# 99 units kept between two layers, and a ring of 14 units instead of 16

## The chip, the cores and the metric

The kernel runs on one core of one Trainium2 chip. The metric is the time of one execution on the device in microseconds. Three runs of the kernel before took 2572.51, 2572.63 and 2572.84 us; the median is 2572.63 us.

## The reference

Two layers with the same weights, one after the other, for two sequences of one new token each. A layer is a grouped-query attention over a cache and then a gated feedforward, each with a layer norm ahead and a residual around it:

```python
q = (x @ wq).reshape(B, Sq, Hq, Dh)                     # 32 query heads, 8 key heads, Dh 128
scores = einsum("bhqd,bhkd->bhqk", q, k) * Dh ** -0.5   # 32768 keys
o = einsum("bhqk,bhkd->bhqd", softmax(scores), v)
x = x + o @ wo
h = gelu(x @ w_gate) * (x @ w_up)                       # 512 -> 1792
x = x + h @ w_down
```

Everything is float32. Keys and values of both sequences are 537 MB, and a layer reads all of them, so the two layers read them twice unless something of the first pass is still on the chip when the second begins.

## The kernel before

**Units and places.** The on-chip memory is one tile `M` of 110 units; a unit is 128 partitions x 512 floats, 262,144 bytes. Units 0 to 31, 32 to 63 and 64 to 95 are three slots (A, B, C) for half a head's keys or values of one sequence (32 units). Units 96 to 107 are the zone for weights; 106 and 107 also hold the exponentials of the attention, 108 and 109 their transposes and other short-lived data.

**What sets the order of transfers.** All loads go through one list, `plan`, in the order in which they are needed. `pump` (L107) issues them on SyncE's queue from the head of the list while the units that the head wants are free; a head that has to wait holds back all behind it. `free` (L125) is called after the instructions that read a unit last, and calls `pump`. So transfers run in order, and each is issued as soon as its place has been read for the last time. TensorE consumes the units in the same order.

**The turn between the layers.** Layer 1 walks the pairs of head and sequence backwards, so the last pair of layer 0 is the first of layer 1, and what of its keys and values is still in `M` is not loaded again. Before the change these are 97 units: both value halves (64), the first `KC1` = 28 units of the second key half, which stay in slot C, and the last `NPS` = 5 units of the first key half (27 to 31), which are copied to PSUM banks ahead of the softmax (L500, L505) and later back to `M` by `store` (L537). The other 4 units of the second key half are loaded again as ("k1",), the other 27 of the first as ("k0", 1).

**The ring.** While those units are held, the weights of feedforward 0 (gu 28 units, wd 14) and the query weights of layer 1 (wq7 4 units, then wq 28) pass through what is left: 16 units in four places of 4, used in the order 104, 92, 96, 100 (`RING`, `PL`, `ring_stream` L166). The place 92 lies in slot C, behind the 28 kept units. A transfer into a place waits for the products that read its occupant.

**The consumers.** `feedforward(0)` makes 28 products from gu (L403), the gelu, and 14 products from wd (L452). Then `center` (L262) normalises, and `query_unit` (L281) makes the query of head 7 from wq7. After that seven groups m = 0 to 6 follow: each makes 4 query products for the other heads (L281, bank 7) and then scores four kept key units (L305, bank 5), in `early` portions of 0, 4, 4, 4, 4, 4 and the rest. Each scored key unit is freed for the first key half of the same pair, which comes as transfers of 8, 8, 8 and 3 units. Behind the groups stand the query copy and gather of all other heads (L285, L289), the scores of the reloaded k1 units and the scores of the first key half, in which the units that were kept in PSUM come after the first 24.

Of the kernel before, what the change touches and what calls it, by code (L numbers as in the profile page):

```python
# [28 lines left out]
CH = 32  # L29
# [3 lines left out]

NU = 110
SLOT_A, SLOT_B, SLOT_C, ZONE = 0, 32, 64, 96
PL = [96, 100, 104, 92]
U_P0, U_P1, U_PT = 106, 107, 108
XW = 46
XO = 14
# [4 lines left out]
NPS = 5  # L44
KFREE = CH - NPS
RING = [2, 3, 0, 1]
KC1 = 28
NARROW = [6, 1]
NH = 2
NG = P // 16  # L50
# [24 lines left out]
def block_kernel(ctx: ExitStack, tc: tile.TileContext, x, consts, kt, vt, wq, wo, wn, gu, wd, out):  # L75
# [28 lines left out]
    def add(key, src, u, n):  # L104
        plan.append((key, src, u, n))
# [30 lines left out]
    def cols(a, lo, n):  # L136
        return a[:, lo * U:(lo + n) * U]
# [17 lines left out]
    def stream(name, l, src, total, cuts, places):  # L155
        lo = 0
        where = {}
        for n, u in zip(cuts, places):
            add((name, l, lo), cols(src, lo, n), u, n)
            for i in range(n):  # L160
                where[lo + i] = ((name, l, lo), u + i)
            lo += n
        assert lo == total
        pieces[(name, l)] = where

    def ring_stream(name, l, src, total, at):  # L166
        cuts, places, n = [], [], 0
        while n < total:
            cuts.append(min(4, total - n))
            places.append(PL[RING[at % 4]])  # L170
            n += 4
            at += 1
        stream(name, l, src, total, cuts, places)

# [14 lines left out]
    for l in range(2):  # L189
        if l == 0:  # L190
            stream("wq", 0, wq, 32, (16, 16), (SLOT_C, SLOT_C + 16))
            ring = [SLOT_A, SLOT_B, SLOT_C]
            todo = sequence(orders[0], 0)
            roles = [ring[(len(todo) - 4 + i) % 3] for i in range(3)]
        else:
            last0, last1, lastv = roles
            ring = [lastv, last0, last1]
            g, b = orders[1][0]
            assert last1 == SLOT_C
            add(("wq7",), cols(wq, 28, 4), ZONE + 2, 4)  # L200
            stream("wq", 1, wq, 28, (4, 2, 2, 4, 4, 4, 2, 2, 4), [ZONE + i for i in (6, 10, -4, -2, 2, 6, 10, -4, -2)])
            add(("k1",), cols(kt[b, g, 1], KC1, CH - KC1), ZONE + 2, CH - KC1)
            stream("k0", 1, kt[b, g, 0], KFREE, (8, 8, 8, 3), [last1 + i for i in (0, 8, 16, 24)])
            g, b = orders[1][1]
            chunk("k", 1, g, b, 0, last1, (8, 8, 16))
            chunk("k", 1, g, b, 1, lastv, (16, 16))
            chunk("v", 1, g, b, 0, last0)
            add_wo(1, g)
            chunk("v", 1, g, b, 1, last1)
            todo = sequence(orders[1][2:], 1)  # L210
        for i, (g, b, nm_, h) in enumerate(todo):
            if nm_ == "w":
                add(("wn", l, g), wn[l], ring[i % 3], NC)
                continue
            last = i == len(todo) - 1
            second = (g, b) == orders[l][orders[l].index((g, b))] and orders[l].index((g, b)) % 2 == 1
            if nm_ == "v" and h == 1 and second and not last:
                add_wo(l, g)
            chunk(nm_, l, g, b, h, ring[i % 3], (8, 8, 8, 4, 4) if last else (CH,))
            if last:  # L220
                add_wo(l, g)
        if l == 0:
            ring_stream("gu", 0, gu, 28, 0)
            ring_stream("wd", 0, wd, 14, 7)
        else:
            stream("gu", 1, gu, 28, (8, 8, 8, 4), [ring[(len(todo) - 3) % 3] + 8 * i for i in range(4)])
            stream("wd", 1, wd, 14, (4, 4, 2, 2, 1, 1), [ring[(len(todo) - 2) % 3] + i for i in (0, 4, 8, 10, 12, 13)])
# [75 lines left out]
    def score_unit(S, w, i, u, start, stop):  # L303
        c, t = divmod(i, 4)
        nc.tensor.matmul(S[32 * t:32 * t + 32, :], w[:, 28 - 4 * c:60 - 4 * c], mem(u), start=start, stop=stop)  # L305
# [215 lines left out]
    g, b = last  # L521
# [7 lines left out]
    k1 = pieces[("k", 0, g, b, 1)]  # L529
    where = pieces[("wq", 1)]  # L530
    S0, S1, A1 = bank[0], bank[5], bank[1]
    todo, s = deque(range(KC1)), 0
    early = [0, 4, 4, 4, 4, 4, CH]
    C0 = SLOT_C + KFREE
    held = {30: C0 + 1, 31: C0 + 2, 27: C0 + 3, 28: C0 + 4, 29: C0}
# [5 lines left out]
    for m in range(7):  # L541
        for j in range(4):
            key, u = where[s]
            at(key)
            query_unit(X, m, j, u, m == 0, m == 6)
            s += 1
        for j in range(4):
            free(where[s - 4 + j][1])
        if m == 0:
            query_gather(mem(U_PT), Q7, 7, 1)  # L550
            w = window(g, b)
        for j in range(min(early[m], len(todo))):
            i = todo.popleft()
            score_unit(S1, w, i, k1[i][1], i < 4, False)
            free(k1[i][1])
        if m == 5:
            store(30, True)
            store(31, False)
    store(27, True)
    store(28, False)  # L560
    store(29, True)
    restart()
    query_copy(X, mem(U_PT + 1))
# [2 lines left out]
    where = pieces[("k0", 1)]  # L566
    u = at(("k1",))
    for i in range(KC1, CH):
        score_unit(S1, w, i, u + i - KC1, False, True)
    free(u, CH - KC1)  # L570
    peak(S1, 1)
    seq = list(range(24)) + [30, 31, 27, 28, 29] + [24, 25, 26]
    left = {i % 4: i for i in seq}
# [67 lines left out]
```

## Time and profile before

| | |
|---|---|
| median of three runs | 2572.63 us |
| the profiled execution | 2573.33 us, of it the span 2571.2 us |
| PE busy | 1359.9 us (53%) |
| DVE, ACT busy | 139.1 us (5%), 83.5 us (3%) |
| read from HBM | 1103.98 MB, 429 GB/s over the span |
| SyncE's DMA queue | 99.6% of the 16 engines' span |
| granted TensorE clock, mean | 0.742 |

The span is the time from the first to the last instruction. In the answers for windows the columns after the stretch are the busy times of PE, of its weight loads, DVE, ACT and POOL with their numbers of instructions, then the granted clock, the DMA share and GB/s. A float32 product over one unit stands as two instructions in the trace, so "x8" is four units. In rows of the timeline the two numbers ahead are start and duration, and the bracket behind says how long the engine sat idle before and what ended that.

### The profile page before, as it was taken

The page shows a single profiled execution, that of the slowest core. Times are in us where ns is not written, and L with a number is a line of the kernel's source. Part 1 is how long each engine was busy: PE and PEld are TensorE (multiplying, and loading weights), DVE is VectorE, ACT ScalarE, POOL GpSimd, SP SyncE. Part 2 cuts the span into 40 slices and gives each one's busy share as a digit, 9 for nine tenths or more (in the row PEclk, how much of TensorE's full clock was granted, in tenths as well). Part 3 has the DMA queues.
Part 4 walks back from the last instruction along what each step waited for, and adds up shares of the span by engine and source line. Part 5 has one row for each costly group of instructions (what it writes and reads, how often), then busy time and mean ns, then how long its engine had stood idle before and what let it go on. Part 6 is the DMA issues. An engine that isn't in the chain of part 4 may idle for free.

```text
span 2571.2 us, 20235 instructions
## 1 busy us (share of the span) xinstructions
PE 1359.9 (53%) x9444; PEld 385.1 (15%) x9444; DVE 139.1 (5%) x459; ACT 83.5 (3%) x191; POOL 3.8 (0%) x12
## 2 busy tenths in 40 slices
PE   4554545555445554464576454454455544554556
PEld 1111111111111111111122111111111111111112
DVE  0000000000000000000011000000000000000001
ACT  0000000000000000000010000000000000000000
POOL 0000000000000000000000000000000000000000
PEclk8777777777777777777798777777766777777778
DMA  9999999999999999999999999999999999999998
GB/s 425 426 436 437 428 436 431 433 431 438 428 435 434 429 436 429 436 430 435 423 408 438 431 432 437 426 436 433 431 436 431 434 432 435 428 437 431 434 429 368
DMA packets 27771, 1105.34 MB, mean 430 GB/s; under 512 B 3208, under 2 KB 3464, under 8 KB 5000
## 3 DMA queue, kind: packets, MB, share of 16 engines
q1 hardware_dynamic: 27400, 1103.97, 99.6%
q8 instruction: 74, 1.21, 0.2%
q10 hardware_dynamic: 288, 0.09, 0.0%
q14 instruction: 9, 0.07, 0.0%
HBM read 1103.98 MB, written 0.07 MB: 429 GB/s over the span
## 4 chain that ended last, share of the span: by engine, by line
DMA 67%; PE 23%; another core or an unknown queue 9%; issue 0%; ACT 0%; DVE 0%; SPq 0%; DVEq 0%
DMA M<-in_vt 57%; PE bank L350 16%; DMA M<-in_kt 7%; PE bank L305 5%; DMA M<-in_gu 3%; DMA M<-in_wq 1%; PE bank L371 0%; PE bank L403 0%; DMA M<-in_wd 0%; ACT M L359 0%; PE bank L361 0%; PE bank L452 0%; PE bank L333 0%; DVE oT L364 0%
## 5 line engine op out<-in xcount | busy, mean ns | idle before, releaser
L305 PE MATMUL bank<-M,qw 128*32 128x512 f32 x4096 | 589.2, 737 | 546.8 <-DMA M<-in_kt 546.8
L350 PE MATMUL bank<-M 128*16 128x512 f32 x4096 | 583.9, 733 | 508.4 <-DMA M<-in_vt 508.4
L305 PEld LDWEIGHTS bank<-M,qw 128*32 128x32 f32 x4096 | 142.8, 132 | 980.4 <-DMA M<-in_kt 584.6
L350 PEld LDWEIGHTS bank<-M 128*16 128x16 f32 x4096 | 137.4, 112 | 928.2 <-issue 914.3
L308 DVE TENSOR_REDUCE sm<-bank 128x1 f32<-128x512 f32 x64 | 44.3, 692 | 1124.9 <-PE bank L305 1124.9
L330 ACT ACTIVATE M<-bank,sm 128x512 f32<-128x512 f32 x64 | 43.4, 683 | 1230.7 <-DVE sm L325 1230.7
L333 PE MATMUL bank<-cst,M 128*128 128x128 f32 x256 | 51.1, 348 | 42.3 <-ACT M L330 42.0
L364 DVE TENSOR_REDUCE oT<-bank 128x4 f32<-128x64 f32 x32 | 7.2, 225 | 1120.6 <-PE bank L361 1120.6
L359 ACT ACTIVATE M<-bank,sm 128x512 f32<-128x512 f32 x32 | 22.0, 687 | 1139.2 <-PE bank L350 1139.2
L334 DVE COPY M<-bank 128x512 f32<-128x512 f32 x64 | 43.9, 692 | 60.8 <-PE bank L333 60.8
L333 PEld LDWEIGHTS bank<-cst,M 128*128 128x128 f32 x256 | 37.0, 176 | 52.6 <-ACT M L330 52.6
L361 PE MATMUL bank<-cst,M 128*128 128x128 f32 x128 | 21.0, 286 | 25.9 <-ACT M L359 25.9
L403 PE MATMUL bank<-M,xw 128*32 128x512 f32 x112 | 24.4, 830 | 10.7 <-DMA M<-in_gu 10.1
L324 PE MATMUL bank<-cst,sm 128*128 128x128 f32 x32 | 10.3, 323 | 35.1 <-DVE sm L323 35.1
L338 PEld LDWEIGHTS bank<-cst,sm 128*128 128x128 f32 x128 | 23.1, 253 | 0.0
L361 PEld LDWEIGHTS bank<-cst,M 128*128 128x128 f32 x128 | 13.4, 140 | 55.3 <-ACT M L359 55.3
L338 PE MATMUL bank<-cst,sm 128*128 128x4 f32 x128 | 21.1, 270 | 0.0
L281 PE MATMUL bank<-M,xw 128*32 128x512 f32 x128 | 19.0, 673 | 3.1 <-DMA M<-in_wq 2.4
L371 PE MATMUL bank<-M,oT 128*2 128x512 f32 x120 | 16.6, 592 | 5.1 <-DVE oT L364 5.1
L259 PE MATMUL bank<-cst,xin 128*2 128x128 f32 x32 | 5.0, 308 | 23.2 <-DMA cst<-in_consts 23.2
L324 PEld LDWEIGHTS bank<-cst,sm 128*128 128x128 f32 x32 | 4.3, 133 | 64.2 <-DVE sm L323 64.2
L330 ACT ACTIVATION_READ_ACCUMULATOR M<-bank,sm 128x1 f32 x64 | 12.5, 196 | 0.0
(73 smaller groups left out, 136.3 us busy)
## 6 DMA issues: line engine op xcount, KB each, us to landing
M<-in_wo SPq DMA_DIRECT2D x14, 1024.0 KB, 51.0
M<-in_vt SPq DMA_DIRECT2D x6, 2048.0 KB, 43.1
M<-in_kt SPq DMA_DIRECT2D x3, 4096.0 KB, 19.5
M<-in_kt SPq DMA_DIRECT2D x5, 2048.0 KB, 13.6
M<-in_wq SPq DMA_DIRECT2D x2, 4096.0 KB
M<-in_gu SPq DMA_DIRECT2D x8, 1024.0 KB, 8.6
M<-in_wq SPq DMA_DIRECT2D x6, 1024.0 KB, 7.9
M<-in_gu SPq DMA_DIRECT2D x3, 2048.0 KB, 37.8
```

Source lines behind the costliest of these rows:

```text
L281: nc.tensor.matmul(Q[32 * k:32 * k + 32, :], xw[:, k, XO - 2 * g:XO - 2 * g + 32], mem(u), start=start, stop=stop)
L305: nc.tensor.matmul(S[32 * t:32 * t + 32, :], w[:, 28 - 4 * c:60 - 4 * c], mem(u), start=start, stop=stop)
L308: nc.vector.tensor_reduce(mx[:, h:h + 1], S, axis=AX.X, op=OP.max)
L330: nc.scalar.activation(p[h], S[h], AF.Exp, bias=bias, scale=SCALE, accum_out=ls[:, h:h + 1])
L333: nc.tensor.transpose(S[h][:, k * P:(k + 1) * P], p[h][:, k * P:(k + 1) * P], ident)
L334: nc.vector.tensor_copy(mem(U_PT + h), S[h])
L338: nc.tensor.matmul(X[:, P:P + REP], ls[:, h:h + 1].to_broadcast([P, P]), mask, start=(h == 0), stop=(h == 1))
L350: nc.tensor.matmul(acc[32 * t:32 * t + 16, :], mem(U_PT + h)[:, k * P + 32 * t + 16 * e:k * P + 32 * t + 16 * e + 16], mem(u), start=(h == ...
L359: nc.scalar.activation(md, acc, AF.Copy, scale=linvc)
L361: nc.tensor.transpose(X[:, c * P:(c + 1) * P], md[:, c * P:(c + 1) * P], ident)
L371: nc.tensor.matmul(W[32 * t:32 * t + NB, :], oT[:, t, :], mem(u + t - lo), start=(t > 0 and first), stop=final)
L403: nc.tensor.matmul(G[v][32 * t:32 * t + 32, :], xw[:, k, XO:XO + 32], mem(un), start=(k == 0), stop=(k == KC - 1))
```

## The change

99 units are kept: `KC1` is 30, so 30 units of the second key half stay in slot C, and two instead of four are loaded again. Two units less are left for the ring, which now has places of 4, 2, 4 and 4 units at 104, 94, 96 and 100 (`SIZE`). gu passes in pieces of 4, 2, 4, 4, 4, 2, 4, 4, and wd in 4, 2, 4, 4. wq7 and wq get other places in the same units, and so other occupants to wait for.

```diff
-PL = [96, 100, 104, 92]
+PL = [96, 100, 104, 94]
+SIZE = [4, 4, 4, 2]
-KC1 = 28
+KC1 = 30
@@ ring_stream
-            cuts.append(min(4, total - n))
-            places.append(PL[RING[at % 4]])
-            n += 4
+            i = RING[at % 4]
+            cuts.append(min(SIZE[i], total - n))
+            places.append(PL[i])
+            n += SIZE[i]
             at += 1
@@ the plan of layer 1
-            add(("wq7",), cols(wq, 28, 4), ZONE + 2, 4)
-            stream("wq", 1, wq, 28, (4, 2, 2, 4, 4, 4, 2, 2, 4), [ZONE + i for i in (6, 10, -4, -2, 2, 6, 10, -4, -2)])
-            add(("k1",), cols(kt[b, g, 1], KC1, CH - KC1), ZONE + 2, CH - KC1)
+            add(("wq7",), cols(wq, 28, 4), ZONE + 8, 4)
+            stream("wq", 1, wq, 28, (4, 4, 4, 2, 2, 4, 4, 4), [ZONE + i for i in (-2, 2, 6, 10, -2, 0, 4, 8)])
+            add(("k1",), cols(kt[b, g, 1], KC1, CH - KC1), ZONE - 2, CH - KC1)
...
-            ring_stream("wd", 0, wd, 14, 7)
+            ring_stream("wd", 0, wd, 14, 8)
@@ the turn between the layers
-    todo, s = deque(range(KC1)), 0
+    first = [*range(18), 28, 29, *range(18, 28)]
+    ends = {i % 4: i for i in [*first, 30, 31]}
+    todo, s = deque(first), 0
...
-            score_unit(S1, w, i, k1[i][1], i < 4, False)
+            score_unit(S1, w, i, k1[i][1], i < 4, ends[i % 4] == i)
...
-    store(27, True)
-    store(28, False)
     store(29, True)
...
     for i in range(KC1, CH):
-        score_unit(S1, w, i, u + i - KC1, False, True)
+        score_unit(S1, w, i, u + i - KC1, False, ends[i % 4] == i)
     free(u, CH - KC1)
+    store(27, True)
+    store(28, False)
     peak(S1, 1)
```

The units that come back from PSUM go to 91 to 95. Before, 92 to 95 were ring units by then. Now 92 and 93 are kept key units 28 and 29, which are therefore scored by group 5, ahead of `store(30)` and `store(31)`; and 94 and 95 hold the reloaded k1 units, so `store(27)` and `store(28)` stand behind their scores.

SyncE's queue from the output projection of layer 0 to the first key half of layer 1, before (128x512 is one unit, so 128x2048 is four):

```order
L119 DMA M<-in_wo 128x2048
L119 DMA M<-in_gu 128x2048 x7
L119 DMA M<-in_wd 128x2048 x3
L119 DMA M<-in_wd 128x1024
L119 DMA M<-in_wq 128x2048 x2
L119 DMA M<-in_wq 128x1024 x2
L119 DMA M<-in_wq 128x2048 x3
L119 DMA M<-in_wq 128x1024 x2
L119 DMA M<-in_wq 128x2048
L119 DMA M<-in_kt 128x2048
L119 DMA M<-in_kt 128x4096 x3
```

and in the changed kernel:

```order
L120 DMA M<-in_wo 128x2048
L120 DMA M<-in_gu 128x2048
L120 DMA M<-in_gu 128x1024
L120 DMA M<-in_gu 128x2048 x3
L120 DMA M<-in_gu 128x1024
L120 DMA M<-in_gu 128x2048 x2
L120 DMA M<-in_wd 128x2048
L120 DMA M<-in_wd 128x1024
L120 DMA M<-in_wd 128x2048 x2
L120 DMA M<-in_wq 128x2048 x4
L120 DMA M<-in_wq 128x1024 x2
L120 DMA M<-in_wq 128x2048 x3
```

The pieces are cut otherwise, with the same sums for gu, wd and wq; the row that follows there is `M<-in_kt 128x1024`, two units where four stood.

PE at the end of the groups, before (bank 7 collects the queries, bank 5 the scores of the second key half, bank 0 those of the first; L259 and L289 are the residual and the query gather):

```order
L281 MATMUL bank7_81<-M_63,xw_65 32x512 x4
L305 MATMUL bank5_79<-M_63,qw0_66 32x512 x8
L259 MATMUL bank6_80<-cst_64,xin_73 2x128 x4
L289 MATMUL bank7_81<-cst_64,M_63 128x14 x4
L305 MATMUL bank5_79<-M_63,qw0_66 32x512 x4
L305 MATMUL bank0_74<-M_63,qw0_66 32x512 x32
```

and in the changed kernel, where the same lines are numbered two higher:

```order
L283 MATMUL bank7_81<-M_63,xw_65 32x512 x4
L307 MATMUL bank5_79<-M_63,qw0_66 32x512 x10
L261 MATMUL bank6_80<-cst_64,xin_73 2x128 x4
L291 MATMUL bank7_81<-cst_64,M_63 128x14 x4
L307 MATMUL bank5_79<-M_63,qw0_66 32x512 x2
L307 MATMUL bank0_74<-M_63,qw0_66 32x512 x32
```

Two of the 32 scores moved from behind the gather to ahead of it.

ScalarE in the same place, before (L285 copies the queries, L539 is `store`):

```order
L285 COPY M_63<-bank5_79 128x512
L539 COPY M_63<-bank0_74 128x512
L539 COPY M_63<-bank2_76 128x512
L539 COPY M_63<-bank4_78 128x512
L285 COPY M_63<-bank7_81 128x512
```

and in the changed kernel:

```order
L287 COPY M_63<-bank5_79 128x512
L543 COPY M_63<-bank0_74 128x512
L543 COPY M_63<-bank4_78 128x512
L287 COPY M_63<-bank7_81 128x512
L543 COPY M_63<-bank2_76 128x512
```

The copy from bank 2, which is unit 27, moved behind the query copy; on VectorE the copy from bank 3, unit 28, moved likewise behind the query gather's scaling and ahead of the maximum of the second key half.

## The prediction

> **What bounds the kernel now.** I read the page's head first, for the DMA share, then its chain of waits, then the stage that the change touches (from about 1262 us to 1375 us) by windows and by timeline.
>
> ```profile
> span 2571.2 us, 20235 instructions
> DMA  9999999999999999999999999999999999999998
> DMA packets 27771, 1105.34 MB, mean 430 GB/s; under 512 B 3208, under 2 KB 3464, under 8 KB 5000
> q1 hardware_dynamic: 27400, 1103.97, 99.6%
> DMA 67%; PE 23%; another core or an unknown queue 9%; issue 0%; ACT 0%; DVE 0%; SPq 0%; DVEq 0%
> ```
>
> The transfer engines are busy in all forty slices, and the one queue of SyncE fills 99.6% of their time with 1103.97 MB. PE is on the chain with 23%, but only as what frees a buffer for the next transfer. So the time is bytes over rate, and a change counts if it alters the bytes or lets the queue run dry. The stage between the layers is no exception:
>
> ```profile
> 1289.00:1336.00 47.00, 35.38 (x244) 10.31 (x240) 7.81 (x34) 5.63 (x13) 1.70 (x3) 0.93 1.00 405
> 600.00:800.00 200.00, 103.07 (x723) 29.09 (x719) 11.14 (x35) 5.72 (x14) 0.00 (x0) 0.74 1.00 433
> ```
>
> The last two columns are the DMA share and GB/s. The ring stage has a share of 1.00 like the attention stage, at 405 against 433 GB/s: never dry, a little slower per byte. Single arrivals there can be read off PE, which waits for each piece:
>
> ```profile
> 1293.04 1.06 PE L403 MATMUL bank<-M,xw 128*32 128x512 f32 x8
> 1295.52 1.94 PE L403 MATMUL bank<-M,xw 128*32 128x512 f32 x8 [1.41 <-DMA M<-in_gu]
> 1305.43 1.47 PE L403 MATMUL bank<-M,xw 128*32 128x512 f32 x7 [0.57 <-DMA M<-in_gu]
> 1324.31 1.07 PE L281 MATMUL bank<-M,xw 128*32 128x512 f32 x8 [0.56 <-DMA M<-in_wq]
> 1334.56 1.07 PE L281 MATMUL bank<-M,xw 128*32 128x512 f32 x8 [0.55 <-DMA M<-in_wq]
> ```
>
> From 1293.04 to 1305.43 five pieces of 4 units arrive, 2.48 us each, so 0.62 us a unit; from 1324.31 to 1334.56 sixteen units, 0.64 us each. PE needs 1.06 us for 4 units at the full clock and 1.94 us at half; the windows inside those two rows show the clocks (the figure ahead of the last two):
>
> ```profile
> 1293.10:1294.00 0.90, 0.90 (x8) 0.10 (x8) 0.02 (x2) 0.00 (x0) 0.70 (x1) 1.00 1.07 428
> 1295.60:1297.40 1.80, 1.80 (x8) 0.12 (x8) 0.00 (x0) 0.00 (x0) 0.00 (x0) 0.50 1.01 414
> ```
>
> **The change part by part.** *The two units.* The last kt transfer of the old second key half shrinks from 4 units to 2. All other sizes add up as before, so 2 x 262,144 bytes leave the queue. At 0.62 to 0.64 us a unit that is 1.24 to 1.28 us, at the page's 430 GB/s 1.22 us. I take **1.25 us**, since the transfer lies in this stage. The number of transfers from wo up to the first 8-unit kt piece is the same (7 + 4 + 10 + 1 = 22 before, 8 + 4 + 9 + 1 = 22 now), so a cost per transfer would not move.
>
> *Does the gain reach the end?* After the ring the first key half streams in:
>
> ```profile
> 1341.94 1.92 PE L305 MATMUL bank<-M,qw 128*32 128x512 f32 x16 [1.32 <-DMA M<-in_kt]
> 1346.84 3.54 PE L305 MATMUL bank<-M,qw 128*32 128x512 f32 x16 [2.98 <-DMA M<-in_kt]
> 1351.75 3.68 PE L305 MATMUL bank<-M,qw 128*32 128x512 f32 x32 [1.37 <-DMA M<-in_kt]
> 1373.62 38.25 DMA M<-in_vt
> ```
>
> PE waits 1.32 us for the first piece of it. Arriving 1.25 us sooner uses that up almost wholly, but PE still waits 2.98 us at the next piece, so the end of the key half, and with it the softmax, the 128 value products and the vt transfer of 1373.62, come 1.25 us sooner with the queue. That vt transfer took 38.25 us to land for about 20 us of its own bytes, so nothing runs dry there.
>
> *The smaller ring.* A transfer is safe while enough is queued ahead of it. The page gives issue to landing:
>
> ```profile
> M<-in_gu SPq DMA_DIRECT2D x8, 1024.0 KB, 8.6
> M<-in_wq SPq DMA_DIRECT2D x6, 1024.0 KB, 7.9
> M<-in_wd SPq DMA_DIRECT2D x5, 1024.0 KB, 8.3
> ```
>
> Less its own 2.48 us, a 4-unit piece had 5.4 to 6.1 us of work ahead of it. A ring shorter by two units leaves 4.2 to 4.9 us. What is needed shows only at the start of the program, where the queue is empty: the first row is the first issue, the others are the packets from 0.7 to 1.7, to 1.8 and to 2.8 us:
>
> ```profile
> 0.73 0.86 SPq L119 DMA_DIRECT2D M<-in_wq  x2
> DMA packets 0, 0.00 MB, mean 0 GB/s; under 512 B 0, under 2 KB 0, under 8 KB 0
> DMA packets 3, 0.10 MB, mean 89 GB/s; under 512 B 0, under 2 KB 0, under 8 KB 0
> DMA packets 16, 0.52 MB, mean 250 GB/s; under 512 B 0, under 2 KB 0, under 8 KB 0
> ```
>
> So the first packets start 1.0 us after the issue, and all 16 engines have one about 2.0 us after it. I take 2.0 us as the need; 4.2 us covers it.
>
> *The narrowest place* is the third wq piece. Before, wq7 lay on 98 to 101, and 16 units (wq7 and the four pieces behind it) could be issued ahead of the second normalisation. Now wq7 lies on 104 to 107, and the piece for 102 to 105 must wait until wq7's products are done. Only 12 units (wq7 and two pieces) are ahead: 12 x 0.62 = 7.4 us from the landing of the last wd piece. What runs in that time:
>
> ```profile
> 1314.19 0.09 PEld L452 LDWEIGHTS bank<-M,hT 128*2 128x2 f32 x2 [1.07 <-DMA M<-in_wd]
> 1316.46 0.60 ACT L264 ACTIVATE M<-bank 128x512 f32<-128x512 f32 x1 [6.86 <-PE bank L452]
> 1318.41 1.07 PE L281 MATMUL bank<-M,xw 128*32 128x512 f32 x8 [0.43 <-DVE xw L269]
> 1319.54 0.33 SPq L119 DMA_DIRECT2D M<-in_wq  x1
> ```
>
> Before, the landing is at 1314.19 and the release at 1319.54, 5.35 us later. The landing does not move in the new kernel (46 units from wo to wd in both), but its last piece has 4 units, 1.1 us of PE at the full clock, 1.9 at half. From the normalisation to the release stand 1319.54 - 1316.46 = 3.1 us. So the release comes 4.2 to 5.0 us after the landing, and 7.4 less that leaves **2.4 to 3.2 us** ahead (before, with 16 units: 9.9 - 5.35 = 4.6 us). That is above 2.0, so I price the stall at nothing; the cover is wq7 and the two pieces behind it. The later pieces (released by query products, then four score products) keep some 3.7 us.
>
> The other side of the bound: the trace shows no piece with less than 4.6 us ahead, so by it alone 4.6 could be needed. Then the narrow place loses up to 2.2 us, the three turns of the ring before it, at 4.2 us, 0.4 each, and the one and a half behind it, at 3.7 us, 0.9 each: 4.8 us in all, and with the 1.25 saved 2576.2. I keep to the start of the program, since it shows the very thing, and leave this end a small chance.
>
> The Trainium skill, in DMA: Bandwidth & Descriptors, "Anatomy of one DMA", puts about 2.0 us of fixed cost on a transfer and bytes over 436 GB/s on top (fitted there on GpSimd's path). If the queue paid that per piece, 1 MB would take about 4.4 us by an estimate from that page; this trace has 2.48 us, so it is hidden behind the pieces queued ahead. Where only 2.4 us are queued the rule leaves 0.4 us to spare, and the sum would stay the same by either.
>
> *The moved work.* The scores of the kept units are the same 32, two of them moved from behind the query gather to the last group: 2 x 0.27 = 0.5 us later for the gather, 0.5 us less after it. The copies of units 27 and 28 move behind the last of them, because units 94 and 95 are now theirs after the transfer:
>
> ```profile
> 1335.68 0.69 DVE L539 COPY M<-bank 128x512 f32<-128x512 f32 x1 [1.77 <-PE bank L281]
> 1337.43 0.59 ACT L539 COPY M<-bank 128x512 f32<-128x512 f32 x1 [1.21 <-PE bank L305]
> 1340.68 0.69 DVE L308 TENSOR_REDUCE sm<-bank 128x1 f32<-128x512 f32 x1 [0.66 <-PE bank L305]
> ```
>
> On ACT one 0.59 us copy goes behind the query copy, with nothing waiting behind it until the exponentials. On DVE a 0.69 us copy goes ahead of the maximum of 1340.68, which then ends about 1342.1; its reader, the softmax, starts after the other maximum, behind products that run from 1351.75 to 1355.4. The copied units are read after 24 others, past 1351. Both have some 10 us of cover: **0**. Without it, they would cost 1.3 us.
>
> **Sum:** profiled execution 2573.33 us (span 2571.2 and 2.1 us around it) - 1.25 = 2572.1, span 2569.95. That execution lies 0.70 us above the median of the timed runs, 2572.63, so the forecast for the median is **2571.4 us**, 0.05% less.
>
> **The rivals.** *The narrow place runs dry once.* If a free ring place needs a microsecond more than the start of the program shows, because the engines are loaded, the third wq piece leaves a hole of about 1.2 us and the saving is gone: 2572.6. For it: 2.4 us is a lead that no row shows to be enough. Against: share 1.00 throughout, and 1 to 2 us at the start.
>
> *Slower: the ring starves at half clock.* The windows granted 0.60 at 1312 to 1315 us, 0.83 to 1318, 1.00 after that:
>
> ```profile
> 1312.00:1315.00 3.00, 1.99 (x10) 0.36 (x12) 0.17 (x1) 0.00 (x0) 0.00 (x0) 0.60 1.02 419
> 1315.00:1318.00 3.00, 2.14 (x10) 0.69 (x6) 0.10 (x1) 0.69 (x2) 0.00 (x0) 0.83 1.01 410
> 1318.00:1321.00 3.00, 2.59 (x21) 0.90 (x21) 0.76 (x7) 0.59 (x1) 0.69 (x1) 1.00 1.01 408
> ```
>
> PE has 2.1 us of work (four query and four score products) for every 4 units, which arrive in 2.56. In a window of 3 us at half clock it does 1.5 us of that work where 2.5 are due, and falls 1.0 us behind. The 0.4 us to spare at the narrow place and the 1.25 saved are gone in the second such window, and from there it decides; three of them in a row make a hole of 3.0 - 0.4 = 2.6 us, 1.35 more than is saved: 2572.63 + 1.35 = **2574.0 us**. Against it: PE has more to do just there now (four instead of two units behind the last wd landing), and the clock came back in time before. The Trainium skill, TensorE: Matmul & The Clock Gate, Part 1, gives 1.2 against 2.4 GHz and about 3.4 us of sustained work to come back; 1.94 against 1.06 us agree with the ratio, and by that rule one stretch is the likely length, not three.
>
> *The change does not do what it says,* the two units being loaded elsewhere: 2572.6. The order of SyncE's transfers excludes it, so 1%.
>
> **How the numbers follow.** Forecast 0.75 (2570.9 to 2571.9), dry once 0.12, starving 0.06, not done 0.01, the far bound of 2576.2 0.03; 0.03 for a gain over 2 us that I cannot name. Runs of this kernel agree within 0.33 us, and the profiled one lay 0.7 us above them. The range goes from 2570.3 (1.28 saved, and a microsecond of such difference) to 2573.5, which takes in the first rival with that difference and leaves out starving, the far bound and the unnamed gain, 12 in 100. About 0.2%, 5.1 us, is what a measurement of this kernel can tell from no change; neither 1.25 us saved nor 3.5 lost comes near, so same 0.97, faster 0.01, slower 0.02.
>
> **What would show it.** Right: HBM read 1103.46 MB; DMA share 1.00 from 1289 to 1336 us; the first products of the key half 1.2 us sooner than 1341.94; the third wq transfer after wq7 landing about 5 us after its issue. Wrong: a landing there that comes later than the pieces queued ahead account for, PE waiting over 3 us for in_wq, or a clock of 0.5 past 1318 us.

## The result, and the profile after

The changed kernel takes 2575.4 us, the median of 21 runs from 2572.10 to 2580.14; the kernel before, run beside it, takes 2572.51 us (21 runs, 2572.01 to 2575.8). The ratio is 1.0013, 95% interval 1.0007 to 1.0018. The change costs some 3 us where 1.25 us less was forecast. That is within the 0.2% named beforehand as no change, but outside the predicted range of 2570.3 to 2573.5.

The head of the page after, of an execution of 2578.63 us. The GB/s row has 40 slices of 64.4 us; the ring is in the 21st.

```profile
span 2576.7 us, 20229 instructions
GB/s 424 436 427 435 432 432 435 430 438 428 433 436 430 433 435 428 435 432 434 417 363 430 440 431 433 432 434 431 435 435 429 434 434 430 435 433 430 434 434 367
...
HBM read 1103.45 MB, written 0.07 MB: 428 GB/s over the span
```

The bytes fell as worked out, from 1103.98 to 1103.45 MB. The 21st slice moves 363 GB/s, the lowest of all forty; the slices around it have 417 and 430. The same stretch as in the prediction, in a window and then in pieces of 3 us (the last three columns are the granted clock, the DMA share and GB/s):

```profile
1289.00:1336.00 47.00, 36.01 (x196) 11.63 (x188) 6.79 (x32) 4.68 (x11) 1.69 (x3) 0.76 0.93 349
...
1288.00:1291.00 3.00, 2.12 (x10) 0.11 (x8) 0.22 (x1) 0.49 (x1) 0.00 (x0) 0.50 0.74 304
1291.00:1294.00 3.00, 2.39 (x14) 1.45 (x14) 0.70 (x6) 0.20 (x2) 0.00 (x0) 0.50 0.95 354
1294.00:1297.00 3.00, 3.00 (x18) 1.02 (x14) 0.33 (x3) 0.00 (x0) 0.69 (x1) 0.50 0.66 213
...
1300.00:1303.00 3.00, 1.92 (x12) 0.14 (x4) 1.44 (x4) 1.32 (x3) 0.00 (x0) 1.00 0.74 262
...
1330.00:1333.00 3.00, 3.00 (x24) 0.68 (x20) 0.00 (x0) 0.00 (x0) 0.00 (x0) 0.66 0.90 317
```

Before, these 47 us had a share of 1.00, 405 GB/s and a clock of 0.93. Now the transfer engines run dry again and again, and TensorE is at half clock for long stretches from 1288 us on. 349 in place of 405 GB/s over 47 us are 6.5 us of transfer; the profiled execution lies 7.2 us over the forecast of 2571.4. So the loss is in this stage. The chain of waits through it (start, length, what; a DMA row runs from issue to landing):

```profile
1288.56 1.93 PE bank L373 x8
...
1292.95 1.94 PE bank L405 x8
...
1295.40 3.11 PE bank L405 x14
1298.53 7.38 DMA M<-in_gu
1305.95 3.63 PE bank L405 x10
1309.61 5.63 DMA M<-in_wd
...
1316.35 8.29 DMA M<-in_wq
...
1332.74 5.83 DMA M<-in_wq
```

In this stage PE and the queue release each other in turn: products at half clock (1.93 and 1.94 us for 4 units) free a place late, the transfer into it starts late, the next products wait for it. The timeline of PE shows the largest of these holes and the start of the key half:

```profile
1301.05 1.05 PE L405 MATMUL bank<-M,xw 128*32 128x512 f32 x4 [0.19 <-DMA M<-in_gu]
...
1305.95 5.25 PE L405 MATMUL bank<-M,xw 128*32 128x512 f32 x14 [3.85 <-DMA M<-in_gu]
...
1348.82 1.74 PE L307 MATMUL bank<-M,qw 128*32 128x512 f32 x8 [0.54 <-DMA M<-in_kt]
```

The piece of 1298.53 follows the one that PE takes at 1301.05. It was issued 2.5 us before that landed, a lead that the prediction took for safe, and needs 2.48 us for its own bytes. It is there at 1305.95, 4.90 us after the other: **2.4 us of nothing**. The first full key piece comes at 1348.82; in the profile before it was 1341.94.

Below, the *lead* of a transfer is the time from its issue to the landing of the last piece ahead of it, and a *hole* is what its landing comes later than that piece's landing plus its own bytes.

### The profile page after: what moved, and what is told of

It reads as the page before. It is cut to its first block, busy times and chain, and to the rows that moved or that the text cites. A ratio compares the mean times of both kernels' runs of the same rounds, so it can differ in the third digit from the quotient of the medians.

```text
span 2576.7 us, 20229 instructions
## 1 busy us (share of the span) xinstructions
PE 1362.8 (53%) x9444; PEld 386.1 (15%) x9444; DVE 138.9 (5%) x459; ACT 83.4 (3%) x191; POOL 3.8 (0%) x12
## 2 busy tenths in 40 slices
DMA packets 27771, 1104.82 MB, mean 429 GB/s; under 512 B 3208, under 2 KB 3464, under 8 KB 5128
## 3 DMA queue, kind: packets, MB, share of 16 engines
HBM read 1103.45 MB, written 0.07 MB: 428 GB/s over the span
## 4 chain that ended last, share of the span: by engine, by line
DMA 64%; PE 24%; another core or an unknown queue 10%; ACT 1%; issue 0%; DVE 0%; SPq 0%; DVEq 0%
DMA M<-in_vt 55%; PE bank L352 16%; DMA M<-in_kt 6%; PE bank L307 6%; DMA M<-in_gu 2%; DMA M<-in_wd 1%; DMA M<-in_wq 1%; PE bank L373 1%; ACT M L361 0%; PE bank L363 0%; PE bank L386 0%; PE bank L405 0%; PE bank L283 0%; PE bank L335 0%
```

## The experiments

All times are medians (range of the runs) beside the kernel before in the same session, which took 2572.46, 2572.75 and 2572.67 us. All ratios are to it, with 95% intervals.

### The changed kernel once more

No edit.

> The changed kernel once more, unaltered, to see its spread and a second profile. Theory A (TensorE at half clock reads the ring's pieces late, the clock windows lie otherwise in each run, and a ring of 14 units has no reserve for it): times spread again from about 2572 to 2580 us, and a profile near 2572 us shows a granted clock of 1.0 through most of 1285 to 1335 us, one near 2578 us shows 0.5 there. Rival B (the reserve of the smaller ring is too short at any clock): the spread is not tied to the clock, every profile shows the same gaps between landings. Rival C (only the third wq piece behind wq7 runs dry): the lost time lies between 1314 and 1330 us, none ahead of it.

2576.94 us (2571.90 to 2580.22), ratio 1.0012 (1.0003 to 1.0021). The loss is there again, and so is the spread. The lowest runs, 2571.9 here and 2572.1 in the first session, come near the forecast, but they are no lower than the lowest runs of the kernel before beside them (2571.93 and 2572.01). In the profiled execution (2577.22 us) the half clock and the holes stand at other places: the clock is at 1.00 until 1297 us here, and the wd, wq and kt pieces lose the time.

### The smaller ring without the smaller bytes

KC1 stays 28 with the ring of 14; four units are loaded again, as before.

```diff
-KC1 = 30
+KC1 = 28
-            add(("k1",), cols(kt[b, g, 1], KC1, CH - KC1), ZONE - 2, CH - KC1)
+            add(("k1",), cols(kt[b, g, 1], KC1, CH - KC1), ZONE - 4, CH - KC1)
...
-    held = {30: C0 + 1, 31: C0 + 2, 27: C0 + 3, 28: C0 + 4, 29: C0}
+    held = {30: ZONE, 31: ZONE + 1, 27: C0 + 3, 28: C0 + 4, 29: C0}
```

> The ring of the change (14 units, the same places for gu, wd, wq7 and wq), but only 28 units of the second key half are kept and four are loaded again, as before; units 92 and 93 lie idle until then. So only the ring shrinks and the bytes are those of before. If the saved bytes are worth their transfer time (1.25 us) and the ring costs the rest: the changed kernel's time plus 1.25, about 2576.6 us median, 2573 to 2581. If the ring is innocent and keeping the two units (their earlier scores, the later copies) costs the time: 2572.5, as before.

2576.14 us (2573.11 to 2580.08), ratio 1.0015 (1.0006 to 1.0024). The ring alone costs the loss; no part of the kept units in it is seen. Against the changed kernel the median tells nothing within such a spread. The lowest runs, 2573.11 against 2571.90, differ by 1.2 us, what two units were priced at, but that is one run of eleven on each side.

### Which half of the ring

The ring of 14 for the feedforward alone (wq in four places of 4), and for wq alone (gu and wd in four places of 4), both with the bytes of before. The diffs are against the changed kernel and leave out `KC1` = 28, the other places of wq7 and of the reloaded units, and what follows from them.

```diff
-            stream("wq", 1, wq, 28, (4, 4, 4, 2, 2, 4, 4, 4), [ZONE + i for i in (-2, 2, 6, 10, -2, 0, 4, 8)])
+            stream("wq", 1, wq, 28, (4,) * 7, [ZONE + i for i in (-4, 0, 4, 8, -4, 0, 4)])
```

> Only the feedforward's ring shrinks: gu and wd pass through 14 units in places of 4, 2, 4, 4, while wq7, wq and the four reloaded key units use 16 units in four places of 4, and 28 units are kept as before (bytes of before). Theory A and rival B: the loss arises mostly in the feedforward, where a wait for its layer norm and gelu falls into the ring, so 2574 to 2576 us. Rival C (the narrow place is behind wq7): no loss here, 2572.5 us.

```diff
-PL = [96, 100, 104, 94]
-SIZE = [4, 4, 4, 2]
+PL = [96, 100, 104, 92]
...
+            stream("wq", 1, wq, 28, (4, 2, 4, 4, 4, 2, 4, 4), [ZONE + i for i in (8, -2, 0, 4, 8, -2, 0, 4)])
```

> Only the ring of the query weights shrinks: gu and wd pass through 16 units as before the change, wq7 and wq through 14 units in places of 4, 4, 2, 4 with 14 units instead of 16 ahead of the second layer norm, bytes of before. Rival C: the loss of the changed kernel is here, 2575 us or more. Theory A: a smaller part, 2572.5 to 2574 us, since TensorE has more work there and idles less.

Feedforward alone: 2573.65 us (2572.16 to 2576.99), ratio 1.0004 (0.9995 to 1.0013). wq alone: 2574.39 us (2572.35 to 2576.76), 1.0005 (0.9996 to 1.0014). Each interval reaches 1, so no half is shown slower by itself; both medians lie above before, by 0.9 and 1.6 us, and their sum of 2.5 is short of the 3.7 that both together cost. Neither is *the* narrow place by this, with one reserve: with wq alone, 14 units could be issued ahead of the second normalisation, not 12 as in the changed kernel, so the narrowest place of the prediction was widened by two units in that run. The profiled execution of the wq half, 2572.35 us, had no loss, and the same window then reads as before the change:

```profile
1289.00:1336.00 47.00, 34.45 (x248) 10.02 (x244) 8.12 (x34) 5.76 (x13) 1.69 (x3) 0.98 0.99 406
```

### Shorter pieces, so more lead

The changed kernel, but its 14 units are seven places of 2, each freed as soon as its two units are read. The bytes are the same; a piece now has up to 12 units ahead of it.

```diff
+    fine = [104, 106, 94, 96, 98, 100, 102]
...
+    def ring_stream(name, l, src, total):
+        places = [fine[(turn[0] + i) % len(fine)] for i in range(total // 2)]
+        turn[0] += total // 2
+        stream(name, l, src, total, (2,) * (total // 2), places)
```

> The changed kernel with the same 14 ring units used as seven places of 2 instead of 4, 2, 4, 4: gu, wd, wq7 and wq pass in pieces of 2 in one turning order, each freed as soon as its two units are read. When a piece is released, 12 units instead of 10 are queued or waiting ahead, 1.2 us more, and the release comes 0.5 us sooner since two units are read, not four. Theory A and rival B alike: most of the loss goes, 2571.5 to 2573.5 us; A says that a spread stays if the half clock lasts. If short pieces cost by themselves (a fixed cost for each of 20 more transfers), 2576 us or more.

2572.19 us (2571.89 to 2575.13), ratio 1.0002 (0.9993 to 1.0011): the loss is gone from the median, though three of the eleven runs still took 2574.85 to 2575.13. The window and a row of its chain:

```profile
1289.00:1336.00 47.00, 39.91 (x236) 10.80 (x234) 7.48 (x33) 5.27 (x12) 1.69 (x3) 1.00 1.02 405
```

```profile
1297.91 7.80 DMA M<-in_gu
```

The same 14 units and the same products, and the share is back at 1.02. A piece of 2 units takes about 1.27 us for itself, so this one had 6.5 us ahead of it. The space is the same and the loss is gone, so it is not the space as such that the change lacked. The clock was up as well in this execution (1.00 against 0.76), so the window alone does not tell lead from clock; that is the next question.

### Half clock or lead

Products of a zero tile, which change no result, in PE's waits of this stage, to hold the clock up: many (178 more PE instructions, 89 products at two each), then fewer (76 more, 38 products), then the fewer ones in the kernel before.

```diff
+    def warm(n, B):
+        if hot[0]:
+            for _ in range(n):
+                nc.tensor.matmul(B[0:32, 256:384], zero, ident, start=True, stop=True)
...
+                    if t == 0 and v == 0:
+                        warm(3, W)
```

> The changed kernel with TensorE kept from idling between the softmax of the last pair of layer 0 and the end of the wq groups: small products of a zero tile with the identity (128 columns) into free columns of banks stand ahead of each piece's products, 1 to 3 of them, some 0.2 us each at full clock. Everything else is the same. Theory A: granted clock near 1.0 from 1285 to 1340 us, times near the forecast of the change, 2571 to 2573 us, with a spread under 1 us. Rival B (reserve too short at any clock): no gain, 2575 us or more, since the added work makes TensorE later. Rival C: about 2575 as well, with the gap at the third wq piece.

> The changed kernel with fewer small zero products than in the first attempt, which added 28 us of TensorE time and made it late by itself: three of about 0.2 us ahead of the last four arrivals of the values, two in each wait of the output projection and of the normalisation, three ahead of each of the four rows of the first gu products, two ahead of pairs of the wd products, none in the second gu products or the wq groups. They fall into waits for arrivals. Theory A (half clock is what makes the smaller ring fail): granted clock 1.0 from 1285 to about 1320 us, median 2571.3 to 2572.5 us. Rival B (ring too short at any clock): 2575 us or more with the clock at 1.0.

> The same small zero products in the kernel before the change, with its ring of 16. Theory A: nothing to gain but the tail of its spread (single times up to 2575.8), 2572.2 to 2572.6 us. Rival B: 2572.5. If the added work itself makes TensorE late, more than 2573 us.

With many: 2578.99 us (2576.19 to 2580.69), ratio 1.0024 (1.0015 to 1.0032). That was a bad tool: the profile shows a clock of 0.96 with a DMA share of 0.88 over 1289 to 1336 us, presumably because the zero products stood ahead of real ones and released places late. With fewer: 2573.94 us (2572.11 to 2577.39), ratio 1.0003 (0.9994 to 1.0012). By the medians 1.5 to 3 us of the loss are regained, but the interval overlaps those of the changed kernel (1.0007 to 1.0018 and 1.0003 to 1.0021), so how much is only loosely known. In the kernel before they leave the median where it was: 2572.48 us, 0.9998 (0.9989 to 1.0007); its highest run is 2573.47 instead of 2576.24, of 11 runs against 33. So half clock seems to carry a part of the loss, mainly where the ring is short. The rest is seen in the profiled execution with fewer zero products (2577.16 us), window and chain:

```profile
1289.00:1336.00 47.00, 36.25 (x268) 15.24 (x262) 6.80 (x32) 4.69 (x11) 1.69 (x3) 0.96 0.97 376
```

```profile
1318.57 1.07 PE bank L293 x8
...
1319.66 7.37 DMA M<-in_wq
```

This is the place that the prediction called the narrowest: the third wq piece, issued behind wq7's products, here at the full clock (1.00 from 1318 to 1327 us, and 1.07 us for 4 units). Its lead is 3.0 us, inside the predicted 2.4 to 3.2. With 2.48 us for its own bytes it should have landed 5.45 us after its issue; it took 7.37. The hole of **1.9 us** is there with a lead 1 us above the supposed need, and with the clock up.

### The needed lead by itself

The kernel before, with ring and bytes untouched. In the attention stage, where the queue is otherwise always full, the next pair's first key half may at ten places be issued only when r units of the running value half are still to come. The edit also has the ten value halves and the key halves behind them come in shorter pieces; those lines are left out here.

```diff
+    behind = {(0, 2): 2, (0, 4): 4, (0, 6): 6, (0, 8): 8, (0, 10): 10, (1, 2): 12, (1, 4): 10, (1, 6): 8, (1, 8): 6, (1, 10): 4}
...
+                if h == 1 and (l, g, b) in tested and i == CH - tested[(l, g, b)] - 2:
+                    old = pieces[("k", l, g, b, 1)]
+                    nc.tensor.matmul(X[0:32, 256:384], zero, mem(old[0][1])[:, :P], start=True, stop=True)
+                    for j in range(CH):
+                        free(old[j][1])
```

> What lead does a transfer need? At ten pairs of the attention stage, where the queue is otherwise always full, the place of the next first key half is given free only when r units of the value half are still to land, r being 2, 4, 6, 8 and 10 in the first layer (from the first tested pair on) and 12, 10, 8, 6 and 4 in the second. PE waits for each of the last pieces, so the release comes when about r units of 0.62 us less some 1 us are still under way: leads of about 0.5, 1.6, 2.8, 4.0, 5.2 and 6.5 us. Prediction's theory (2.0 us from the program's start are enough): a hole of about 1.5 us at r = 2 and 0.4 at r = 4, none from r = 6 on; 4 us in all over the ten pairs, about 2576. Theory of the loaded queue (about 4.7 us are needed): holes of some 4, 3, 2 and 0.7 us at r = 2, 4, 6 and 8, none at 10 and 12; about 19 us in all, near 2590. Either way the hole should shrink by 0.6 us for each unit more of lead; if it jumps about at equal leads in the two layers, the need is no fixed number.

2589.45 us, one run, 16.8 over before. The total is what the theory of 4.7 us said, but its parts are not. From 2 us ahead of each of the ten issues to 6 us behind it, with r = 2, 4, 6, 8, 10, then 12, 10, 8, 6, 4:

```profile
257.58:265.58 8.00, 4.49 (x30) 1.03 (x22) 0.23 (x1) 0.69 (x1) 0.00 (x0) 0.99 0.69 268
417.91:425.91 8.00, 4.48 (x30) 0.85 (x26) 0.23 (x1) 0.69 (x1) 0.00 (x0) 1.00 0.81 311
577.32:585.32 8.00, 4.59 (x26) 0.74 (x18) 0.00 (x0) 0.51 (x1) 0.00 (x0) 0.84 0.90 353
735.26:743.26 8.00, 3.92 (x22) 0.63 (x22) 0.00 (x0) 0.00 (x0) 0.00 (x0) 0.79 0.97 400
892.49:900.49 8.00, 2.92 (x22) 0.66 (x18) 0.00 (x0) 0.00 (x0) 0.00 (x0) 0.77 0.98 408
1514.65:1522.65 8.00, 2.45 (x26) 0.60 (x18) 0.00 (x0) 0.00 (x0) 0.00 (x0) 0.93 0.96 409
1674.57:1682.57 8.00, 2.95 (x22) 0.67 (x18) 0.00 (x0) 0.00 (x0) 0.00 (x0) 0.75 0.96 393
1833.73:1841.73 8.00, 4.16 (x26) 0.64 (x23) 0.00 (x0) 0.00 (x0) 0.00 (x0) 0.82 0.95 387
1994.34:2002.34 8.00, 4.81 (x26) 0.74 (x18) 0.00 (x0) 0.52 (x1) 0.00 (x0) 0.81 0.82 333
2154.89:2162.89 8.00, 5.05 (x30) 1.19 (x26) 0.23 (x1) 0.69 (x1) 0.00 (x0) 0.80 0.79 308
```

Against the 409 GB/s of r = 12 the windows lack 2.8 us of bytes at r = 2 (lead 0), 1.9 and 2.0 at r = 4 (lead 1.3), 1.1 and 1.5 at r = 6 (2.4 to 2.6), 0.2 and 0.4 at r = 8 (3.7), 0 to 0.3 at r = 10 (4.8). So the queue begins to lose bytes below a lead of some **4 us**, gently: some 0.6 to 0.7 us for each microsecond of lead that is missing, not one for one as the expectation had it.

The landings tell another story. Rows of PE's timeline at r = 2, and at the second r = 6:

```profile
259.52 0.12 PEld L364 LDWEIGHTS bank<-M 128*16 128x16 f32 x4 [0.23 <-DMA M<-in_vt]
259.58 2.45 SPq L120 DMA_DIRECT2D M<-in_kt  x5
...
271.69 3.64 PE L319 MATMUL bank<-M,qw 128*32 128x512 f32 x16 [2.97 <-DMA M<-in_kt]
```

```profile
1996.34 2.41 SPq L120 DMA_DIRECT2D M<-in_kt  x5
1998.73 3.05 PE L364 MATMUL bank<-M 128*16 128x512 f32 x12 [2.42 <-DMA M<-in_vt]
...
2008.65 1.92 PE L319 MATMUL bank<-M,qw 128*32 128x512 f32 x16 [1.87 <-DMA M<-in_kt]
```

The key pieces of 4, 4 and 8 units follow the last value piece. At 0.62 us a unit the 16 need 9.9 us. At r = 2, 259.52 to 271.69 are 12.2 us: 2.3 late. At r = 6, 1998.73 to 2008.65 are 9.9: with a lead of 2.4 us the landing is on time, although that window lacks 1.5 us of bytes. By the landings in the trace the first key piece is 1.1 and 1.0 us late at r = 4 and on time at the other r = 6, so here the last engine loses one microsecond for each that is missing. The windows of 1 us at r = 2 say how both can be:

```profile
257.00:258.00 1.00, 0.96 (x8) 0.13 (x8) 0.00 (x0) 0.00 (x0) 0.00 (x0) 1.00 0.67 266
258.00:259.00 1.00, 0.79 (x8) 0.23 (x5) 0.00 (x0) 0.00 (x0) 0.00 (x0) 1.00 0.34 139
259.00:260.00 1.00, 1.00 (x8) 0.23 (x5) 0.00 (x0) 0.00 (x0) 0.00 (x0) 1.00 0.00 0
260.00:261.00 1.00, 0.56 (x4) 0.00 (x0) 0.00 (x0) 0.40 (x1) 0.00 (x0) 1.00 0.57 98
261.00:262.00 1.00, 0.66 (x4) 0.42 (x4) 0.00 (x0) 0.29 (x1) 0.00 (x0) 1.00 0.75 270
```

The last value piece lands at 259.5, but a third of the engine time is idle from 257 and two thirds from 258. **The 16 engines are not in step:** the first of them have done their share some 2 us ahead of the last, and the landing shows only the last. The trace has 16 landing records for each transfer, read here as one for each engine's share: those of the last value piece run from 257.56 to 259.47 us, those of the first key piece behind the drain from 263.88 to 264.28. After the issue at 259.58 it takes 2.4 us until all move data again. So the last engine needs a lead of 2.4 us, and the first needs 2.4 plus the 2 us that it is ahead. The first figure is what the prediction read as 2.0 us from the start of the program, where no engine is ahead of another (the first piece there has its records within 0.5 us).

A landing on time does not mean that nothing was lost. At the second r = 6 the records of the key pieces are 0.6 us apart; the value half that lands at 2058.2 us has them 1.8 us apart again, and it lands 20.5 us after its predecessor, where 19.4 are usual.

### What short pieces cost

The kernel before with its 16 units in eight places of 2, and the changed kernel in seven places of 2 with the fewer zero products.

```diff
+    fine = [104, 106, 92, 94, 96, 98, 100, 102]
```

> The kernel before with its 16 units in eight places of 2: bytes and reserve as before, only the pieces are shorter (some 19 transfers more). Theory that a piece of 2 units costs its queue about 0.035 us over half a piece of 4: 0.7 us slower than before, 2573.2, without any hole. Theory that the short pieces cost nothing: 2572.6. If this kernel runs no slower than before, the changed kernel in seven places of 2 (2572.19) has lost its saving elsewhere.

> Both remedies together: 99 units kept, the ring of 14 in seven places of 2, and the zero products in PE's waits that hold the clock up. Theory that half clock and the short reserve make all of the loss: no slow execution is left, 1.25 us saved less 0.7 us for the short pieces, about 2572.0 with a spread under 0.6 us, ratio about 0.9998. Theory that something else made the spread: executions of 2574 to 2580 go on.

Eight places of 2: 2574.0 us (2572.97 to 2575.19), ratio 1.0003 (0.9994 to 1.0012). Its page has 30075 packets and before has 27771:

```profile
DMA packets 30075, 1105.34 MB, mean 430 GB/s; under 512 B 3464, under 2 KB 3720, under 8 KB 9352
```

2304 more are 16 more transfers, not the 19 expected: the ring needs 37 pieces of 2 where there were 21 pieces, and each has 128 packets of data and 16 small ones (256 more stand under 512 B). Medians differ by 1.3 us and the lowest runs by 1.0, so a transfer more costs an estimated 0.06 to 0.08 us, about twice the 0.035 expected, if all of that is the transfers; the interval reaches 1. Seven places of 2 ran at 2572.19, 1.1 (lowest) to 1.8 us (median) under eight places of 2: at equal pieces the two kept units seem worth what was forecast, and the short pieces take it back. The two were timed in different sessions, and their ratios, 1.0002 and 1.0003, do not separate them, so this is not shown. With the zero products: 2572.18 us (2571.91 to 2573.20), ratio 0.9998 (0.9989 to 1.0007). No execution above 2573.2 is left, and no gain over before that could be measured. None of the variants beats the kernel before.

### All in one row

GB/s over 1285 to 1345 us of each profiled execution, against its time:

| kernel | GB/s | clock | profiled, us |
|---|---|---|---|
| before | 406 | 0.94 | 2573.33 |
| before, fewer zero products | 411 | 1.00 | 2572.19 |
| wq half | 406 | 0.97 | 2572.35 |
| seven places of 2, zero products | 400 | 1.00 | 2572.28 |
| seven places of 2 | 402 | 0.97 | 2572.02 |
| eight places of 2 | 395 | 0.89 | 2574.00 |
| smaller ring, bytes of before | 387 | 0.94 | 2574.69 |
| changed, fewer zero products | 380 | 0.97 | 2577.16 |
| feedforward half | 371 | 0.86 | 2576.99 |
| changed, again | 360 | 0.80 | 2577.22 |
| changed | 353 | 0.80 | 2578.63 |
| changed, many zero products | 340 | 0.97 | 2580.07 |

60 us at 353 instead of 406 GB/s are 7.8 us of transfer, at 340 are 9.8, at 380 are 3.8; less the 1.25 us of the kernels that load two units less, the times follow within 2 us. The clock alone does not order them. What is moved in this stretch decides, and half clock is one way to move less.

## Why the prediction was wrong

**Right: the two units.** 1103.45 MB against the expected 1103.46, and worth an estimated 1.2 us (lowest runs with 28 and 30 units in the same ring) or 1.1 to 1.8 us (short pieces with 14 and 16). The moved scores and copies, priced at nothing, show no cost: seven places of 2 has them all and is not slower than the kernel before. That the gain reaches the end if nothing runs dry is not shown: the lowest runs of the changed kernel, 2571.9 and 2572.1, are no lower than those of the kernel before.

**Wrong, and the step that failed: the needed lead.** "I take 2.0 us as the need; 4.2 us covers it." The start of the program was the wrong place to read it. There, all 16 engines are idle and begin together; in the ring the landing records of a transfer are some 2 us apart, and 8 us at its start (below), and the first engine runs dry that much earlier. Measured in the attention stage, the need is 2.4 us for the last engine and about 4 for none to idle; in the ring, leads of 2.5 and 3.0 us cost 2.4 and 1.9 us. The lead itself held only at the full clock: in gu it was 4.1 to 5.4 us in the second profile of the changed kernel, but 1.6 to 2.5 us for three pieces in the first, where PE at half clock released the places late. The other bound, 4.6 us, was the better one; it gave 4.8 us lost and 2576.2, and the medians were 2575.4 and 2576.94. It stood in the text, and was given 3 chances in 100. Its places were not those where the profiled executions lost their time, so that the total fits is in part chance. The trace of before held no lead below 4.6 us, and that should have kept the two ends nearly equal in weight.

The Trainium skill, DMA: Bandwidth & Descriptors, "Anatomy of one DMA", with about 2.0 us of fixed cost for a transfer, left 0.4 us to spare at the narrow place. Under that rule the third wq piece could not be late at a lead of 3.0 us. It was, by 1.9: here the measurement differs from what I made of the page, and the rule is no measure of what a loaded queue must hold.

**Overlooked in a row that was there.** "Never dry" was read from a mean of 47 us. Three of them, in the profile before, in windows of 3 us:

```profile
1288.00:1291.00 3.00, 1.88 (x16) 0.80 (x14) 0.24 (x2) 0.69 (x2) 0.00 (x0) 1.00 0.84 320
```

A mean of 1.00 over 47 us, in which single windows reach 1.06, can hold a window of 0.84. The ring of 16 had no reserve to give.

The landing records say why the share falls just there. In the profile before, those of the gu piece issued at 1270.83 us run from 1287.60 to 1295.47, 7.9 us apart, and four of the 16 stand ahead of 1288.3. The next piece was issued at 1289.55. So some engines had run dry before that issue, though the landing, by which the prediction counted, was still 5.9 us away. In the profile after, the same records run from 1286.06 to 1294.11, and the next issue is at 1290.50, so those engines wait longer. The spread had grown over the kernel, from 0.5 us in the first piece to 3.6 us at 600 us; behind this first drain it is 4 to 2 us before and 3 to 0.5 us after.

**The narrow place: right in one profile, wrong in price.** With fewer zero products the third wq piece had 3.0 us of lead where 2.4 to 3.2 were worked out, and lost 1.9 us, not nothing. In the two profiles of the changed kernel itself its lead was 4.4 us, with nearly nothing lost, and 1.3 us at half clock, with 1.1 lost. So it was one place of several. In the first of these profiles the losses began before it, in gu and wd, and went on behind it; a landing that is late makes the next release late.

**The rival "dry once", 2572.6, and the rival "starves at half clock", 2574.0.** The second is the nearest in mechanism: PE at half clock frees too late, and that is in the chain (1.93, 1.94 and 3.11 us ahead of the issue at 1298.53). It was placed at wq only, in three windows; it began with wo and gu at 1288 us. One reason was in the timeline of before: I gave PE 1.06 us for 4 units at full clock throughout, but the products of gu's second part take longer.

```profile
1300.59 1.88 PE L403 MATMUL bank<-M,xw 128*32 128x512 f32 x8 [1.09 <-DMA M<-in_gu]
1302.96 1.90 PE L403 MATMUL bank<-M,xw 128*32 128x512 f32 x8 [0.49 <-DMA M<-in_gu]
```

At half clock that is over the 2.48 us of a piece (3.63 us for ten instructions, five units, in the chain after, so 2.9 for four), so the release falls behind the queue for as long as the clock stays down. That was three windows in a row, 1288 to 1297 us, with PE busy for 2.12, 2.39 and 3.00 of each 3 us. The Trainium skill, TensorE: Matmul & The Clock Gate, Part 1, asks for about 3.4 us of sustained work before the clock comes back; these windows agree with it, as the clock came back at about 1297.9 us, after 4.9 us of unbroken work. But "one stretch is the likely length", as I drew from it, did not follow: ahead of that work PE stood still in between for the normalisation (0.81 us for ScalarE, 0.36 us for VectorE). And the clock is not all of it: with the clock held up, in the profile until 1327 us, about half of the loss stayed (2573.94 against the forecast of 2571.4, of a loss of 4.0 to 5.5 us).

**What would show it wrong** did: landings later than the pieces ahead account for, and a granted clock of 0.50 between 1327 and 1330 us. The predicted PE wait of over 3 us came for in_gu (3.85 us), not for in_wq.

**Open.** The lead explains where pieces are lost, not how much each loses. In the profiled execution of the changed kernel a lead of 2.5 us cost 2.4 us at 1298.53, where the single drains at a lead of 2.4 to 2.6 us cost the landing nothing. The windows around that issue:

```profile
1299.00:1300.00 1.00, 0.55 (x6) 0.16 (x8) 0.00 (x0) 0.00 (x0) 0.00 (x0) 1.00 1.01 410
1300.00:1301.00 1.00, 0.86 (x8) 0.00 (x0) 0.00 (x0) 0.05 (x1) 0.00 (x0) 1.00 0.47 180
1301.00:1302.00 1.00, 0.95 (x4) 0.14 (x4) 0.55 (x2) 0.45 (x2) 0.00 (x0) 1.00 0.80 229
1302.00:1303.00 1.00, 0.11 (x2) 0.00 (x0) 0.90 (x3) 0.81 (x2) 0.00 (x0) 1.00 0.96 377
```

Half of the engine time is idle from 1300 to 1301, up to 2.5 us after the issue, and the share is whole again only at 1302, 3.5 us after it: here a transfer took longer to reach its engines than in the attention stage (2.4 us). The landing records say so too: those of the piece ahead are only 0.5 us apart, those of this one stand 4.7 to 7.4 us after its issue, where the drained pieces of the attention stage with leads up to 2.6 us had theirs at 4.2 to 5.1 us. Why this refill was slower, no run told apart. Also open is how the 16.8 us of the lead test divide: 10.2 us are bytes missing in the ten windows, 85 more transfers are an estimated 5 to 7 us by the cost above, and that leaves little or nothing.

## What to carry to other kernels

When a ring of buffers is made smaller, work out for each transfer how long before the landing of its predecessor it can be issued, and compare that with the smallest such lead in a profile that runs without holes under the same load, not with the start-up of an idle queue. Where the trace has a landing record for each engine's share, count from the first of them: the landing that releases the consumer is the last. A ring of more and shorter places gives more lead from the same memory, but each transfer seems to have its price (here an estimated 0.06 to 0.08 us), which can eat a gain of 1 us. Read the DMA share in windows of a few microseconds: a mean of 1.00 over a stage can hide that it is already at its limit.

## What was unexpected of the hardware

- The 16 engines of one queue drift apart: some 2 us between the first and the last landing record of a piece at the first tested place of the lead test, and in the kernel before 0.5 us at its start, 3.6 us at 600 us and 7.9 us at the turn. A drain brings them together again, to 0.4 us at a lead of 0. In the lead test a queue starts losing bytes while the last piece ahead is still 4 us from landing, and loses 2.8 us of them when the next issue comes right at the landing.
- After such a drain the landing of the next pieces can be on time (lead 2.4 us) though 1.5 us of bytes were not moved in the window, because the landing goes by the last engine. Some 1.2 us showed about 60 us later, when the engines had drifted apart again.
- A transfer of 512 KB instead of 1 MB costs an estimated 0.06 to 0.08 us more of the queue for each one added, at the same bytes (from medians and lowest runs whose interval reaches no change).
- The granted clock falls to half at different times in executions of the same program (from 1288 us in one profile of the changed kernel, after 1297 in the other). With 16 units of ring, holding the clock up left the median where it was; with 14 the times spread over 8 us, from 2572.1 to 2580.1, and over the 21 runs a lower mean clock goes with a longer time (correlation -0.74; 0.750 with 2572.1, 0.739 with 2580.14).
